# The first batch's Fourier sums in five PSUM banks, zero products in its waits, its later adds beside the first FFN

## The chip, the core and the metric

One core of a Trainium2 chip. The time is device time of one execution in microseconds (us); less is better. The engines are TensorE (PE, with its weight loads as PEld), VectorE (DVE), ScalarE (ACT), GpSimd (POOL) and SyncE (SP, which issues most DMAs). Each engine runs its own instructions strictly in order and waits on semaphores for the others.

## The reference

Three stages on B=4 sequences of S=576 tokens with 512 features, all in float32:

```
x  = softmax(mask128(q k^T / 8) + alibi) v          # 8 heads of 64, window of 128 keys
u  = x + real(fft(fft(x, over tokens), over features))
un = (u - mean(u)) / sqrt(var(u) + 1e-6)
y  = u + relu(un @ w_ch1) @ w_ch2                   # 512 -> 2048 -> 512
out[b, s] = p[e] * (relu(y[s] @ w1[e]) @ w2[e])     # e: one of 8 experts, by a gate that may keep the last e
```

The weights `w_ch1` and `w_ch2` come as 64-bit floats.

## The kernel before

Products that must be exact to float32 are made as three products of split operands: `split(hi, lo, src)` rounds `src` to `hi` on ACT and subtracts on DVE or POOL to get `lo`, and `mm3` multiplies hi by hi (L169), hi by lo (L170) and lo by hi (L171).

**The opening** (`opening()`) treats batch 0 alone, in an order written out by hand for PE, DVE, ACT and POOL. PE starts on products of a zero tile (`warm`, L306). Then comes `attention(0)`: ten units (two groups of four heads, five query tiles), each with score products on PE (L363), a masked scaling and a minimum on DVE (L367, L369, L371), four exponentials on ACT (L378), a transpose on PE (L387) copied by ACT (L391), selections on POOL (L392, L394), value products on PE (L406), a copy on DVE (`ot`, L412 and L414), and a transpose back with a scaling by the reciprocal of the sums into the rows `x` (L426 to L434). The stages of several units overlap.

Then comes `mixing(0)`. A sequence's 576 rows lie as three tile pairs `xs[kt]` (row s beside row 576-s). `fold(kt)` adds and subtracts the pair's halves and then mirrored columns on DVE (L471 to L480); `zprod` multiplies the folded tiles by the table `tab1` on PE (`zps`, L494), summed over kt; ACT copies the sums to `Z` (L498). For each of three row blocks kb, PE multiplies by `tab2` (`pz`, `pc`, L517, L518), ACT copies `pz` (L521), and DVE forms difference and sum (L522, L523) and adds them, straight and mirrored, to the rows x (L527, L528). The first halves of tile pairs 0 and 1 are normalised (`normalise`: statistics L634, a chain of small DVE operations L643 to L663, scaling on ACT L668), transposed and split (`transpose_split`) to `xT`. That is the input of the first FFN.

**The conversion** of the 64-bit weights (`load_weights64`, `values32`): ACT scales the high word (L264), DVE shifts the low word right by 29 (L265), merges the two (L266) and puts the sign in (L267), ACT and POOL split the result into `t1` and `t2` (L165, L166). Pieces go by pairs through two buffers `t64`, each free again when POOL has subtracted. Chunk 0 is converted in the opening, chunks 1 to 3 beside the first FFN.

**The first half of the FFN** (`mlp_first`) runs over nine groups of two row tiles, each with eight hidden blocks: 12 products into `hps`, relu on ACT (`h`, L580) and its rest on DVE (L583), then two `mm3` into `acc`. Beside it run attention and mixing of batches 1 to 3. What goes where is set by lanes, each with a start, a length and a count of steps; a scheduler then orders the engines. A group's successor is normalised at the steps `STEPS` of its FFN. After that come the second FFN half with routing, and the experts.

Of the kernel before, what the change touches and what calls it, by code (L numbers as in the profile page):

```python
# [23 lines left out]
DM = H * D  # L24
# [20 lines left out]
WARM = 24  # L45
FILL = 14
# [16 lines left out]
STEPS = (0, 3, 4, 9, 11)  # L63
# [94 lines left out]
def build(ctx, tc, a, out):  # L158
# [5 lines left out]
    def split(hi, lo, src, eng=None):  # L164
        nc.scalar.copy(hi, src)  # L165
        (eng or nc.vector).tensor_tensor(out=lo, in0=src, in1=hi.bitcast(F32), op=ALU.subtract)  # L166
# [69 lines left out]
    def load_weights64(chunks, i, c, wp, words):  # L236
        q = CB // 2
        ms = []
        for j in range(2):
            ms.append(values32(raws[c][j], words))  # L240
            if j == 0:
                yield
# [6 lines left out]
        for j in range(2):  # L249
            ms.append(values32(raws[c][2 + j], words))  # L250
            if j == 0:
                yield
# [6 lines left out]
    def values32(r, words):  # L259
# [31 lines left out]
    def load_part(b, g, part, pieces=1):  # L291

        t = qk.tile([P, 2, QK], F32, tag="qk", name="qkt")
        n = 2 // pieces
        for x in range(pieces):
            nc.sync.dma_start(out=t[:, x * n:(x + 1) * n], in_=a["qk"][b, g, part, :, x * n:(x + 1) * n])
        v = sm.tile([P, 3, 4 * D], F32, tag="v", name="vt", bufs=QB)
        last["load"] = nc.sync.dma_start(out=v, in_=a["v"][b, g, part].rearrange("p k h d -> p k (h d)"))
        return t, v

    raw0 = load_part(0, 0, 0, 2)
# [5 lines left out]
    ident = keep.tile([P, P], F32, name="ident")  # L307
    nc.sync.dma_start(out=ident, in_=a["ident"])
    turn = cst.tile([P, P], F32, name="turn")
    nc.vector.tensor_copy(turn, ident[:, ::-1])  # L310
    half = keep.tile([P, TM], F32, name="half")
    nc.vector.memset(half, -0.5)
    inner = keep.tile([P, 2], F32, name="inner")
    nc.sync.dma_start(out=inner, in_=a["inner"])
    first = cst.tile([P, P], BF16, name="first")
    nc.sync.dma_start(out=first, in_=a["first"])
    mask = cst.tile([P, P], I32, name="mask")
    nc.sync.dma_start(out=mask, in_=a["mask"])
    bias = cst.tile([P, 2, 4, P], BF16, name="bias")
    nc.sync.dma_start(out=bias, in_=a["bias"].rearrange("p g h x c -> p g (h x) c"))  # L320
    id16 = cst.tile([P, P], BF16, name="id16")
    nc.sync.dma_start(out=id16, in_=a["id16"])
    mixed = [-1]
    xss = {}
# [7 lines left out]
    def attention(b):  # L332
# [108 lines left out]
        for u in range(len(units) + VL + 1):  # L441
# [15 lines left out]
            yield  # L457

    def mixing(b):
        xs = xss.pop(b)  # L460
        rows = [(P, P), (P, P), (33, 32)]
        zin = []

        def fold(kt):
            n, m = rows[kt]
            xa, xb = xs[kt][:, 0], xs[kt][:, 1]
            xf = slab([P, 2, DM], F32, "xf", "m", MB)
            xe, xo = xf[:, 0], xf[:, 1]
            if kt == 0:

                nc.vector.scalar_tensor_tensor(out=xe, in0=xb, scalar=inner[:, 0:1], in1=xa, op0=ALU.mult, op1=ALU.add)  # L471
            else:
                nc.vector.tensor_tensor(out=xe[0:m], in0=xa[0:m], in1=xb[0:m], op=ALU.add)
            o = 64 if kt == 2 else 0
            nc.vector.tensor_tensor(out=xo[o:o + m], in0=xa[0:m], in1=xb[0:m], op=ALU.subtract)
            if kt == 2:
                nc.vector.tensor_copy(xe[32:33], xa[32:33])
                nc.vector.memset(xo[o + 32:o + 33], 0.0)
# [31 lines left out]
        for kb in range(3):  # L510
# [33 lines left out]
            if kb == 2:  # L544
                mixed[0] = b
# [803 lines left out]
```

## Time and profile before

| | |
|---|---|
| median of 3 runs | 980.03 us (977.93 to 981.56) |
| the profiled execution | 980.93 us, its span 978.9 us |
| PE busy | 910.6 us, 93% of the span |
| DVE, ACT, POOL busy | 53%, 38%, 24% |

The span is what the engines' records cover; the 2.0 us around it are start and end of the execution. Times of single instructions are from this one execution. An instruction that follows another of its engine without a pause starts some 0.08 to 0.1 us before the end shown for the other, so starts, not durations, give the pace.

### The profile page before, as it was taken

How to read it: one execution, taken by the hardware profiler on the slowest of the kernel's cores; microseconds unless marked ns; L12 is line 12 of the kernel's file. 1: busy time of each engine (PE TensorE's matmuls, PEld its weight loads, DVE VectorE, ACT ScalarE, POOL GpSimd, SP SyncE). 2: the span in 40 equal slices, each digit the busy share in tenths (PEclk: the TensorE clock that was granted, in tenths of full speed). 3: DMA queues.
4: the chain of work that ended last, by engine and by line, in shares of the span. 5: the costliest groups of instructions: out<-in, count | busy, mean ns of one | idle time of the engine just before them, and what ended most of it. 6: DMA issues, size and time to landing. Idle time of an engine off the chain costs nothing. (4 is left out here: it accounts for less than half of the span.)

```text
span 978.9 us, 16130 instructions
## 1 busy us (share of the span) xinstructions
PE 910.6 (93%) x5878; PEld 752.2 (77%) x5879; DVE 521.8 (53%) x1332; ACT 369.8 (38%) x974; POOL 239.7 (24%) x364
## 2 busy tenths in 40 slices
PE   8868899989999999999999999998979999999993
PEld 4535677667778797889888888887758899988782
DVE  5787866745554658521333435357546545565410
ACT  5635363543553246421111111114235445455410
POOL 2315441231221137310111313123023211222100
PEclk9989799979999999999999999999988999999997
DMA  9923071341312396253444342536167555455100
GB/s 324 378 86 108 1 238 61 121 130 52 114 66 69 120 313 194 65 151 65 108 108 108 85 110 44 120 85 194 57 188 247 186 162 164 165 189 196 64 20 20
DMA packets 109036, 129.14 MB, mean 132 GB/s; under 512 B 16222, under 2 KB 78046, under 8 KB 108884
## 3 DMA queue, kind: packets, MB, share of 16 engines
q1 hardware_dynamic: 83636, 103.95, 33.3%
q0 software_dynamic: 22720, 19.36, 9.1%
q10 hardware_dynamic: 2592, 4.72, 1.3%
q8 instruction: 48, 0.79, 0.3%
q14 instruction: 40, 0.33, 0.1%
HBM read 99.65 MB, written 30.87 MB: 133 GB/s over the span
## 5 line engine op out<-in xcount | busy, mean ns | idle before, releaser
L580 ACT ACTIVATE h<-hps 128x256 fp32r<-128x256 f32 x152 | 58.2, 383 | 262.3 <-PE hps L171 259.0
L583 DVE SCALAR_TENSOR_TENSOR h<-hps,h 128x256 fp32r<-128x256 f32 x152 | 63.8, 420 | 160.0 <-ACT h L580 160.0
L169 PE MATMUL acc<-t,h 128*128 128x512 f32 x304 | 125.8, 416 | 3.0 <-ACT h L580 3.0
L171 PE MATMUL acc<-t,h 128*128 128x512 f32 x304 | 121.7, 400 | 1.5 <-DVE h L583 1.2
L170 PE MATMUL acc<-t,h 128*128 128x512 f32 x304 | 121.9, 401 | 1.0 <-POOL t L166 0.9
L166 DVE TENSOR_TENSOR t<-we,t 128x512 fp32r<-128x512 f32 x128 | 84.5, 694 | 46.9 <-ACT t L165 46.9
L169 PE MATMUL hps<-xT,t 128*128 128x256 f32 x288 | 87.0, 302 | 4.8 <-ACT t L165 3.5
L165 ACT CAST t<-we 128x512 fp32r<-128x512 f32 x128 | 73.4, 618 | 42.4 <-DMA we<-in_w 17.9
L171 PE MATMUL hps<-xT,t 128*128 128x256 f32 x288 | 84.7, 294 | 3.5 <-POOL t L166 3.5
L169 PE MATMUL hps<-xTe,t 128*128 128x320 f32 (+7 forms) x288 | 86.4, 301 | 0.6 <-ACT xTe L165 0.6
L170 PE MATMUL hps<-xTe,t 128*128 128x320 f32 (+7 forms) x288 | 86.0, 299 | 0.0
L171 PE MATMUL hps<-xTe,t 128*128 128x320 f32 (+7 forms) x288 | 85.8, 298 | 0.0
L170 PE MATMUL hps<-xT,t 128*128 128x256 f32 x288 | 83.9, 291 | 0.0
L169 PE MATMUL hps<-xTb,t 128*128 128x256 f32 x288 | 83.6, 290 | 0.0
L170 PE MATMUL hps<-xTb,t 128*128 128x256 f32 x288 | 82.3, 286 | 0.0
L171 PE MATMUL hps<-xTb,t 128*128 128x256 f32 x288 | 82.3, 286 | 0.0
L378 ACT ACTIVATE t<-t,mx 128x128 f32<-128x128 f32 (+1 forms) x160 | 62.6, 393 | 45.7 <-DVE mx L371 41.3
L171 PEld LDWEIGHTS acc<-t,h 128*128 128x128 f32 x304 | 57.8, 190 | 17.9 <-DVE h L583 5.0
L169 PEld LDWEIGHTS acc<-t,h 128*128 128x128 f32 x304 | 58.1, 192 | 14.8 <-ACT h L580 3.2
L169 PEld LDWEIGHTS hps<-xT,t 128*128 128x128 f32 x288 | 56.8, 197 | 12.5 <-ACT t L165 4.4
L170 PEld LDWEIGHTS acc<-t,h 128*128 128x128 f32 x304 | 58.2, 191 | 9.8 <-POOL t L166 2.8
L583 DVE SCALAR_TENSOR_TENSOR hE<-hps,hE 128x256 fp32r<-128x256 f32 (+4 forms) x96 | 30.8, 349 | 62.6 <-ACT hE L580 62.1
(280 smaller groups left out, 2018.3 us busy)
## 6 DMA issues: line engine op xcount, KB each, us to landing
we<-in_w SPq DMA_DIRECT2D x64, 512.0 KB
rw<-in_w_ch SPq DMA_DIRECT2D x32, 512.0 KB
qkt<-in_qk SPq DMA_DIRECT2D x15, 642.0 KB
nd<-xT SPq DMA_DIRECT2D x18, 512.0 KB
xTb<-nd POOLq DMA_DIRECT2D x18, 512.0 KB, 6.8
vt<-in_v SPq DMA_DIRECT2D x16, 384.0 KB
pd<-y ACTq DMA_DIRECT2D x18, 256.0 KB
ub<-ud SPq DMA_DIRECT2D x18, 256.0 KB
```

The costliest lines, as they stand in the source:

```text
L165: nc.scalar.copy(hi, src)
L166: (eng or nc.vector).tensor_tensor(out=lo, in0=src, in1=hi.bitcast(F32), op=ALU.subtract)
L169: nc.tensor.matmul(o, lhsT=wh, rhs=xh, start=start, stop=False, **kw)
L170: nc.tensor.matmul(o, lhsT=wh, rhs=xl, start=False, stop=False, **kw)
L171: return nc.tensor.matmul(o, lhsT=wl, rhs=xh, start=False, stop=stop, **kw)
L378: nc.scalar.activation(t[0:m, j], t[0:m, j], AF.Exp, bias=mx[0:m, j:j + 1], scale=-1.0, accum_out=sums[0:m, j:j + 1])
L580: last["relu"] = nc.scalar.activation(h[:, 0:n], hps[:, 0:n], AF.Relu)
L583: last["rest"] = nc.vector.scalar_tensor_tensor(out=h[:, lo:lo + c1 - c0], in0=hps[:, c0:c1], scalar=0.0, in1=h[:, c0:c1].bitcast(F32), op ...
```

## The change

- The first loads stand in another order: half of the first `qkt`, `first` and `id16` come first. There are 16 warm products instead of 24, and `turn` is made on POOL.
- In attention of batch 0, from its last units on, two products of the zero tile (`spin`, 28 in all) stand behind each transpose and each value product; `FILL`, now 18 products, stands behind the `tab2` products.
- The folds of tile pairs 2 and 1 begin inside attention, pair 0 comes last; the odd half of pair 2 has 32 rows instead of 33, with the single row's copy on ACT and no memset.
- The five sums of `zprod` have five banks of their own (of the score tile, of both FFN sums and of the hidden tile) and are taken in the order 2, 1, 0, the cosine sums first.
- Only two row blocks are combined in the opening, and of each only the half that is normalised there. The other adds, row block 2 and the rows' stores are a lane of their own (`rest`, `REST`).
- `early64` scales the high words and takes the low word's top three bits (from its top byte) on ACT, for all four chunks (32 ACT instructions in the opening; before, 14 of L264 stood there and 2 behind it); DVE's shift L265 is gone.
- `normalise` makes both tiles' `u` first (in the opening one on ACT, one on DVE) and transposes afterwards; it has one step more, so `STEPS` has too.

```
-WARM = 24
-FILL = 14
+WARM = 16
+FILL = 18
+SPIN_ = 2
+REST = (25.5, 4)
-STEPS = (0, 3, 4, 9, 11)
+STEPS = (0, 3, 5, 10, 11, 13)
...
+    def early64(c):
+        for r in raws[c]:
...
+            nc.scalar.activation(w[:, :, :, 1].bitcast(F32), w[:, :, :, 1].bitcast(F32), AF.Copy, scale=BIAS)
+            yield
+            nc.scalar.activation(w[:, :, :, 0], top, AF.Copy, scale=1.0 / 32, bias=-31.0 / 64)
+            yield
...
-        nc.scalar.activation(y.bitcast(F32), y.bitcast(F32), AF.Copy, scale=BIAS)
-        nc.vector.tensor_single_scalar(t, wl, 29, op=ALU.logical_shift_right)
-        nc.vector.scalar_tensor_tensor(out=t, in0=y, scalar=3, in1=t, op0=ALU.logical_shift_left, op1=ALU.bitwise_or)
+        if not small:
+            nc.scalar.activation(y.bitcast(F32), y.bitcast(F32), AF.Copy, scale=BIAS)
+            nc.vector.tensor_single_scalar(wl, wl, 29, op=ALU.logical_shift_right)
+        nc.vector.scalar_tensor_tensor(out=t, in0=y, scalar=3, in1=wl, op0=ALU.logical_shift_left, op1=ALU.bitwise_or)
...
+    def spin(n):
...
+        for _ in range(n):
+            nc.tensor.matmul(idle[0], lhsT=id16, rhs=z16, start=True, stop=True)
...
                 flip(u - FL)
+                if b == 0 and u >= len(units) - 1:
+                    spin(SPIN_)
             if VL <= u < len(units) + VL:
                 values(u - VL)
+                if b == 0 and u >= len(units) - 1:
+                    spin(SPIN_)
...
-        for i, g in enumerate(gs):
-            with behind() if later else nullcontext():
-                un = act.tile([P, DM], F32, tag="u", name="u", bufs=UB)
-                nc.scalar.activation(un, src[i], AF.Identity, scale=v[:, 1, i:i + 1], bias=v[:, 2, i:i + 1])
-                transpose_split(xT, i * P, un)
+        us = []
+        with behind():
+            for i in range(n):
+                us.append(act.tile([P, DM], F32, tag="u", name="u", bufs=UB))
+                nc.scalar.activation(us[i], src[i], AF.Identity, scale=v[:, 1, i:i + 1], bias=v[:, 2, i:i + 1])
+        yield
+        for i, g in enumerate(gs):
+            with behind():
+                transpose_split(xT, i * P, us[i])
...
+        bank = {(0, 0): s2[:, 1], (0, 1): a2[0], (0, 2): s2[:, 0], (1, 0): a2[1], (1, 1): h1}
...
+        zprod(2)
+        words.step(2)
+        folding(1)
+        zprod(1)
+        folding(1)
+        zprod(0, (0,))
...
+        kb0 = combine(xs, Z, 0)
+        next(kb0)
+        kb1 = combine(xs, Z, 1)
+        next(kb1)
+        spin(FILL)
+        nrm = prepare(0, (xs[0][:, 0], xs[1][:, 0]))
+        words.step(8)
...
+        def rest():
+            for kb, it in ((0, kb0), (1, kb1), (2, combine(xs, Z, 2))):
+                for _ in it:
+                    yield
+                store(0, xs, kb)
+                yield
...
+    lanes.append(lane(REST[0], REST[1], 8, late_(rest)))
```

How the order moves is seen at two places. The first is ACT in the opening, from the sums' copies to the copy of the second `pz`. Before (the twelve scalings L264 stand ahead of this, two more in it):

```order
L264 ACTIVATE rw<-rw 128x512 x12
L498 COPY z_743<-zps 128x289
...
L378 ACTIVATE t,sums<-t,mx 128x128 x3
L498 COPY z_743<-zps 128x289
L498 COPY z_742<-zps 128x289
L264 ACTIVATE rw<-rw 128x512
L165 CAST t_797<-t_777 128x4x128
L165 CAST t_797<-t_792 128x4x128
L521 COPY cmb<-pz 128x258 x2
```

And of the change, from the last of the 19 instructions of `early64` (L243, L245 in turn) that stand ahead of the sums' copies, which are now L900:

```order
L243 ACTIVATE rw<-rw 128x512
L900 COPY z_749<-zps 128x289 x2
L541 CAST zn<-zps 1x289
L900 COPY z_750<-zps 128x289 x2
L245 ACTIVATE rw<-rw 128x512
L243 ACTIVATE rw<-rw 128x512
L245 ACTIVATE rw<-rw 128x512
L167 CAST t_786<-t_772 128x4x128 x2
L529 COPY cmb<-pz 128x258
```

The attention of batch 1 (L378) is gone from this stretch, and 22 instructions of `early64` stand ahead of the weights' casts where 14 of L264 stood.

The second place is DVE in the first FFN, behind the rest of its first hidden block (L583, now L634). Before:

```order
L265 TENSOR_SCALAR t_1089<-rw 128x512
L583 SCALAR_TENSOR_TENSOR h<-hps,h 128x256
L266 SCALAR_TENSOR_TENSOR t_1089<-rw,t_1089 128x512
L265 TENSOR_SCALAR t_1118<-rw 128x512
L267 SCALAR_TENSOR_TENSOR t_1089<-rw,t_1089 128x512
L266 SCALAR_TENSOR_TENSOR t_1118<-rw,t_1118 128x512
L267 SCALAR_TENSOR_TENSOR t_1118<-rw,t_1118 128x512
L367 COPY_PREDICATED s<-mask,s 128x4x128
```

And of the change (the conversion is L281 and L282, the moved adds are L535 and L536, the scores' scaling and minimum L397 and L399):

```order
L634 SCALAR_TENSOR_TENSOR h<-hps,h 128x256
L535 TENSOR_TENSOR x<-x,cmb 128x257
L536 TENSOR_TENSOR x<-x,cmb 128x255
L397 SCALAR_TENSOR_TENSOR t<-s,bias 128x512
L281 SCALAR_TENSOR_TENSOR t_960<-rw 128x512
L399 TENSOR_REDUCE mx<-t 128x4
L634 SCALAR_TENSOR_TENSOR h<-hps,h 128x256
L282 SCALAR_TENSOR_TENSOR t_960<-rw,t_960 128x512
L535 TENSOR_TENSOR x<-x,cmb 128x257
L536 TENSOR_TENSOR x<-x,cmb 128x255
L530 TENSOR_TENSOR cmb<-pc,cmb 33x258
```

The conversion of a piece has two rows instead of three, and the adds and more of batch 1's attention stand between them. Between the first and the eighth row of the hidden rest, DVE had 12 of L265, 26 of L266 and L267 and 4 score groups (L369 with L371, most with L367); it now has 22 of L281 and L282, 8 score groups and 10 adds (eight into x, two that form difference and sum).

## Rows read from the trace of the kernel before

**Rows 1.** The page: busy time of the engines.
```profile
PE 910.6 (93%) x5878; PEld 752.2 (77%) x5879; DVE 521.8 (53%) x1332; ACT 369.8 (38%) x974; POOL 239.7 (24%) x364
```
**Rows 2.** Stretches: length; busy PE, PEld, DVE, ACT, POOL (instructions); clock, DMA.
```profile
8.46:45.60 37.14, 30.39 (x312) 21.58 (x311) 28.46 (x71) 24.84 (x97) 13.32 (x29) 1.00 1.03 374
45.60:80.20 34.60, 26.22 (x117) 14.30 (x116) 28.40 (x73) 15.74 (x45) 3.74 (x4) 0.85 0.37 130
80.20:139.50 59.30, 49.82 (x311) 37.72 (x310) 45.61 (x80) 27.89 (x83) 31.29 (x42) 0.88 0.33 106
139.50:200.00 60.50, 58.56 (x461) 42.81 (x460) 41.97 (x95) 29.77 (x115) 15.69 (x36) 1.00 0.33 108
```
**Rows 3.** Timeline of PE to the first FFN (start, duration, idle before).
```profile
1.26 7.37 PE L306 MATMUL warm<-z 128*128 128x512 bf16 x24 [1.26 <-DVE carry L877]
...
45.59 3.18 PE L788 MATMUL fill<-bias,id 128*128 128x512 bf16 x13
...
69.90 1.55 PE L363 MATMUL s<-qkt 64*65 64x193 f32 x8 [5.88 <-DVE v L643]
73.61 1.11 PE L552 MATMUL tps<-ident,u 128*128 128x128 f32 x4 [2.16 <-ACT u L668]
...
80.21 0.39 PE L169 MATMUL hps<-xT,t 128*128 128x256 f32 x1
```
**Rows 4.** Timeline of DVE, from the folds to the normalising.
```profile
46.44 0.75 DVE L471 SCALAR_TENSOR_TENSOR xf<-x,inner 128x512 f32<-128x512 f32 x1
...
53.18 0.42 DVE L480 TENSOR_TENSOR xf<-xf 33x255 f32<-33x255 f32 x1
...
62.11 0.43 DVE L522 TENSOR_TENSOR cmb<-pc,cmb 128x258 f32<-128x258 f32 x1 [1.53 <-ACT cmb L521]
...
62.78 1.36 DVE L527 TENSOR_TENSOR x<-x,cmb 128x257 f32<-128x257 f32 x1
...
67.08 1.27 DVE L634 BATCH_NORM_STATS2 st<-x 128x6 f32<-128x512 f32 x2
...
72.55 0.16 DVE L663 SCALAR_TENSOR_TENSOR v<-mv,v 128x2 f32<-128x2 f32 x1
```
**Rows 5.** Timeline of ACT in the Fourier stage.
```profile
42.08 6.87 ACT L264 ACTIVATE rw<-rw 128x512 f32<-128x512 f32 x12
...
57.85 0.70 ACT L498 COPY z<-zps 128x289 f32<-128x289 f32 x2 [0.21 <-PE zps L494]
...
60.66 1.14 ACT L165 CAST t<-t 128x512 fp32r<-128x512 f32 x2 [1.54 <-DVE t L267]
61.71 0.64 ACT L521 COPY cmb<-pz 128x258 f32<-128x258 f32 x2
...
72.74 0.81 ACT L668 ACTIVATE u<-x,v 128x512 f32<-128x512 f32 x1 [0.59 <-DVE v L663]
```
**Rows 6.** Waits from 80.2 to 139.5 us: in total, times, longest.
```profile
DVE t L265 <- POOL t L166: 9.2, 7, 2.5
PE hps L171 <- POOL t L166: 3.5, 3, 2.3
PE hps L169 <- ACT t L165: 3.5, 3, 1.3
```
**Rows 7.** DVE's conversions from 80.2 to 139.5 us, and a pair of POOL's subtractions.
```profile
L265 DVE TENSOR_SCALAR t<-rw 128x512 uint32<-128x512 uint32 x14 | 11.1, 801 | 9.2 <-POOL t L166 9.2
L266 DVE SCALAR_TENSOR_TENSOR t<-rw,t 128x512 uint32<-128x512 uint32 x14 | 9.5, 698 | 0.0
...
104.03 1.50 DVE L265 TENSOR_SCALAR t<-rw 128x512 uint32<-128x512 uint32 x1 [0.73 <-POOL t L166]
...
61.36 2.50 POOL L166 TENSOR_TENSOR t<-t,t 128x512 fp32r<-128x512 f32 x2 [2.61 <-ACT t L165]
102.72 2.53 POOL L166 TENSOR_TENSOR t<-t,t 128x512 fp32r<-128x512 f32 x2 [1.59 <-ACT t L165]
```
**Rows 8.** Timeline of PE: the transposes of a later group's rows.
```profile
201.85 0.65 PE L552 MATMUL tps<-ident,u 128*128 128x128 f32 x4 [2.45 <-ACT u L668]
```

More of the change, by code (lines that the diff above doesn't have):

```diff
@@ L499, in zprod @@
                 else:
-                    nc.scalar.copy(zn[0:1, 0:K1], ps[0:1, 0:K1])
-                    nc.vector.tensor_tensor(out=zn[32:33, 0:K1], in0=ps[0:1, 0:K1], in1=zn[0:1, 0:K1].bitcast(F32), op=ALU.subtract)
+                    low_row(ps[0:1, 0:K1], slice(0, K1))
         for kt in range(3):
-            fold(kt)
+            for xf in fold(xs, kt):
+                pass
+            zin.append(xf)
             zprod(parts[0], kt)
@@ L732, in conversions @@
     def conversions():
-        for c in range(FA // CB):
-            yield from load_weights64(chunksA, c, c, wpA, lambda: sm.tile([P, 2 * CB], U32, tag="t64", name="t64", bufs=2))
+        for c in range(1, FA // CB):
+            yield from load_weights64(chunksA, c, c, wpA, lambda: sm.tile([P, 2 * CB], U32, tag="t64", name="t64", bufs=2), soon64[c])
     END = object()
@@ L768, in mix, with folding @@
         yield from mixing(b)
+    soon64 = [None] * nA
     conv = conversions()
     def opening():
+        xs = None
+        folds, got = [], {}
+        def folding(n):
+            for _ in range(n):
+                for kt, it in folds:
+                    r = next(it, False)
+                    if r is not False:
+                        if r is not None:
+                            got[kt] = r
+                        break
+        words = Beside()
         for n, _ in enumerate(attention(0)):
@@ L778, in opening @@
                 load_raw(0, wpA)
+                soon64[0] = early64(0)
+                words.add(soon64[0])
             if n == 14:
@@ L781, in opening @@
                     load_raw(c, wpA)
-        attended.add(0)
-        ends = [last[x].ins for x in ("x", "w", "pool")]
-        xs = xss[0]
-        fill = ps_h1.tile([P, DM], F32, tag="h", name="fill")
-        for _ in range(FILL):
-            nc.tensor.matmul(fill, lhsT=id16, rhs=bias[:, 0].rearrange("p h c -> p (h c)"), start=True, stop=True)
-        m = mixing(0)
-        for _ in range(3):
-            next(m)
-        next(conv)
-        next(m)
-        next(conv)
-        next(m)
+                    soon64[c] = early64(c)
@@ new lines, in opening @@
+                    words.add(soon64[c])
+            xs = xss[0]
+            if n == 23:
+                folds.append((2, fold(xs, 2)))
+                folding(1)
+            if n >= 24:
+                words.step(2)
+            if n == 25:
+                folding(1)
+                folds.append((1, fold(xs, 1)))
+            if n == 26:
+                folding(1)
+        attended.add(0)
+        folds.append((0, fold(xs, 0)))
+        folding(1)
+        idle[0] = None
+        h1 = ps_h1.tile([P, DM], F32, tag="h", name="zps")
@@ new lines, in copies @@
+        def copies(cs):
+            for db in range(2):
+                nc.scalar.copy(Z[cs][:, db], bank[cs, db][:, 0:K1])
+        zprod(2)
+        words.step(2)
+        folding(1)
+        zprod(1)
+        folding(1)
+        zprod(0, (0,))
+        words.step(1)
+        folding(1)
+        q = CB // 2
+        room0 = [wraw.tile([P, 4 * CB], U32, tag="r64", name="t64", bufs=RB) for _ in range(2)]
+        place = iter([t[:, x * 2 * CB:(x + 1) * 2 * CB] for t in room0 for x in range(2)])
@@ new lines, in opening, with value @@
+        ms = []
+        def value():
+            ms.append(values32(raws[0][len(ms)], lambda: next(place), True))
+        copies(0)
+        value()
+        low_row(bank[0, 2][0:1, 0:K1], slice(0, K1))
+        zprod(0, (1,))
+        copies(1)
+        value()
+        t1 = wpA.tile([P, 2, 4, CB], F32R, tag="w1", name="t1")
+        for j in range(2):
+            split(t1[:, 0, :, j * q:(j + 1) * q], t1[:, 1, :, j * q:(j + 1) * q], ms[j], nc.gpsimd)
+        kb0 = combine(xs, Z, 0)
+        next(kb0)
```

225 lines of the change are left out of this document (136 added, 89 removed).

## The prediction

> **What bounds the kernel now.** I read the page first: PE is busy for 910.6 us of 978.9 [rows 1], so what can be won lies in the 68.3 us of its idle time and in products that run at a low clock. A table of busy time by stretch says where these are. From 45.6 to 80.2 us PE is busy for 26.22 of 34.6 us, at a granted clock of 0.85 of full speed on average (the levels are 1.2 and 2.4 GHz); from 80.2 to 139.5 for 49.82 of 59.3, at 0.88; from there to 200 for 58.56 of 60.5, at 1.00 [rows 2]. So the Fourier stage of batch 0 and the first FFN lose 8.4 and 9.5 us in idle time and some more in slow products, and behind them PE itself is the bound. What is saved before 139.5 us is kept to the end, if the order behind it stays, and the orders of the two kernels say that it does, but for the steps of the normalising.
>
> Next the timelines of that stage. In the Fourier stage a serial chain sets the end. The folds run on DVE from 46.44 to 53.6 us [rows 4]; the last copies of the sums end on ACT at 58.55; ACT copies the first `pz` only at 61.71, behind two casts for which it had waited 1.54 us (DVE's conversion) [rows 5]. DVE combines from 62.11 to 67.1, normalises until 72.7 [rows 4], ACT scales the first tile from 72.74 [rows 5], and the first FFN product comes at 80.21. In this time PE stands still for 5.88 us before 69.90 and 2.16 before 73.61, and a transposition of four blocks then takes 1.11 us, against 0.65 later [rows 3, 8].
>
> In the first FFN the waits say that PE waits for POOL's and ACT's halves of the converted weights, 3.5 us for POOL alone, and DVE for POOL to free a buffer, 9.2 us in 7 times [rows 6]. The chain there is: POOL subtracts, DVE converts the next pair, ACT rounds it, POOL subtracts.
>
> **The change part by part.** I follow the chain, with the times of before.
>
> *Start.* Eight of 24 warm products go, which take 7.37 us together [rows 3]. The last ones are the fast ones; 13 products of the same width later take 3.18 us, 0.23 each [rows 3], so the eight are worth 1.9 us. The first scores need `first` and `id16`, whose loads move from the fifth and the eighth place to the second and the third, so they need not hold the scores. I take -1.7; bounds 0 (a load is late) and -1.9.
>
> *Zero products in attention.* 28 products of 0.23 us are 6.4 us. PE is idle for 6.7 us of the 37.1 of attention [rows 2], so most of them fill time in which it waits. Where one stands directly ahead of value products whose copy DVE is waiting for, it delays; in the last two units that is two pairs of 0.46. I take +0.9; bounds 0 and +6.4. The clock is 1.00 in all of attention already [rows 2], so there they win nothing.
>
> *Folds.* From the first fold to the last DVE spends 7.2 us behind the last row of attention [rows 4]. Now six of its instructions are left there (two of pair 1, four of pair 0): at the mean of the 14 that stood there, 0.51, they take 3.1 us. Four others, 2.0 us, stand just ahead of the last row; part of that fills idle time of DVE (8.7 us of attention's 37.1 [rows 2]), and I let them push the row by 1.3. The folds end 2.8 us earlier than they did, and 13 of their 15 products need not wait for the last one.
>
> *Copies of the sums.* What is late next is ACT. Ahead of these copies stand 19 instructions of `early64`. No row shows the one with the bytes; its bounds are the 0.35 us of a copy of 289 columns (two in 0.70) and double the 0.57 that the scaling L264 takes (12 in 6.87) [rows 5]. I take 0.57, since it writes as many elements in the same stride. 19 of them are 10.9 us. They start where L264 started at 42.08, some 0.4 us later for the copied row, and so end at 53.4, less 1.7, plus 0.9: 52.6. Four copies and the small one (0.35 each at the pace of the row) end at 54.4 where they ended at 58.55: -4.1 so far. Were the byte form to take double, the nine of them here would add 5.1 us.
>
> *To the first combined block.* Three more of `early64` (1.7 us), two casts (1.05) and the copy of `pz`: it starts at 57.2, against 61.71: -4.5.
>
> *Combining and normalising.* DVE did twelve adds from 62.11 to 67.08 [rows 4]; eight stand there now. One of the twelve took 1.36, the others share 3.6, 0.33 each; with that one kept, the eight take 3.7 us, so the statistics begin at 61.2 (-5.9). From there the chain took 5.6 us to 72.7, with three wide instructions of batch 1's attention within (2.1 us by L266's 0.70 [rows 7], less what overlaps, some 1.8); these are gone: 65.0 (-7.7).
>
> *Scaling, transposing.* Before, the second tile came behind the first, and between them stood a row block's products and adds: 72.74 to 80.21, 7.5 us [rows 3, 5]. Now ACT and DVE scale one tile each (0.81), PE transposes eight blocks, at the slow clock of before 2.2 us [rows 3], and ACT rounds the second (0.6): 3.6 us. The first FFN product comes at 69.0 us, 11.2 earlier. I take the slow transposes because PE still stands idle ahead of them: the 18 zero products (4.1 us) end some 3 us before the scaled tiles do.
>
> *The first FFN.* Gone from DVE between the first and the eighth hidden block are 12 instructions of L265, 0.80 us each on average [rows 7], and four merges of 0.70: 12.4 us. In their place come 10 adds at 0.33 (3.3 us) and the attention of batch 1 that used to stand in the opening, four score groups of three wide instructions at 0.70 (8.4): 11.7. DVE's work is nearly the same; PE's grows by the scores and by row block 2, some 6 us, in a stretch in which it has 9.5 us idle. I take its 59.3 us as unchanged. Bounds: -9.2 (DVE's waits for POOL all go, since other work lies between) and +9.5 (each of the ten adds waits for POOL, below).
>
> *Later groups.* Both scaled tiles now exist before either transposition. One wait of this kind is 2.45 us [rows 8]; but the second transposition now stands nearer to the group's end. I take -0.4; bounds -2.45 and +1.2 (a rounding and a subtraction that come too late once).
>
> Sum: -11.2 + 0 - 0.4 = -11.6 on the profiled execution's 980.93 (2.0 more than its span): 969.3. The execution lies 0.9 above the median of the runs, so in medians 968.4; I say 968.5. A measurement can tell about 0.5%, 4.9 us, from no change.
>
> **The rivals.**
>
> *The port (the first FFN gives half back).* While POOL subtracted from 61.36 to 63.86, an add of x and cmb, both in SBUF, took 1.36 us on DVE where the others go on after 0.33 [rows 4, 7]; L265 took 1.50 beside the pair from 102.72, against a mean of 0.80 [rows 7]. So such an add can be held up by about 0.95, taking a free one at 0.4 with its end. The Trainium skill's page "SBUF — State Buffer" ("Who interferes with whom") has this as a rule: a DVE instruction with two inputs in SBUF, or in its two-port mode, and a POOL instruction that reads SBUF exclude each other for their whole length. By that rule, L281, with both inputs in SBUF, waits behind the second subtraction of a pair just as L265 did. As a mechanism of this kernel: the ten adds move from a stretch with 3.74 us of POOL's work into one with 31.29 [rows 2], and each pair's first L281 stays held up by about 1. If half of the adds are hit, +4.8, and the first FFN takes 64: 973.3. All ten hit, +9.5: 978.0. For it: the 9.2 us of waits show that DVE and POOL take turns. Against it: a pair has one held-up instruction as before and two fewer instructions.
>
> *ACT is the chain.* If the byte form costs double, the nine put the copies off by 5.1 us; the other seven stand ahead of the scaling, where ACT is done at 63.7 in the sum above and is waited for at 65.0. Then all sixteen cost 9.1, less that slack: +7.8, 976.3. For it: 32 instructions on ACT where 14 were; against it: no row says that such a read is slower.
>
> *Nothing comes of it.* The first FFN is fed by the conversion alone; if its chain is not shorter and starts no earlier than POOL's and ACT's other work lets it, the 11 us turn into waits for weights: 978 to 982. Against it: the chain's first pairs follow the same start, as chunk 0's do.
>
> *The other side: slower.* Every two-input DVE instruction of the first FFN pays for POOL: the 24 of L281 and L282 for chunks 1 to 3, and the 10 adds. Held up by 0.95 each beyond what is paid today, the 34 are +32: 1000. It decides from 18 of the 34 on: 17 us is what was won and 4.9 more, 985.6. For it: POOL is busy for half of the stretch; against it: L266, with both inputs in SBUF, has a mean of 0.70 in it [rows 7], so it is hardly ever held up.
>
> *More than forecast.* DVE's waits are filled by the adds and the scores: 9.2 us less, 959.
>
> **How the numbers follow.** Forecast 0.60, with its own range from 964 to 973 (the Fourier chain uncertain by 3 us to either side, the first FFN by 2); the port 0.15; ACT 0.08; nothing 0.07; slower 0.05; more 0.05. Faster by over 0.5% means below 975.1: the forecast, more, and two thirds of the port: 0.75, and a little of ACT, 0.76. Slower means above 985: 0.05, and 0.01 of "nothing". The rest, 0.18, is the same. The range from 962 to 977 takes in the forecast, most of the port and ACT, and leaves out "nothing", "slower" and the best cases, some 0.18.
>
> **What would show it.** The first FFN product near 69 us; ACT's sums' copies at 52 to 53, directly behind `early64` with no idle time ahead of them; the first combine near 57.5; no DVE instruction on conversions but two for a piece; the first FFN 57 to 62 us long with a first L281 of 1.1 us or more over its usual time in each pair; from its end on the same intervals as before. I am wrong if the first FFN takes over 66 us, if the copies of the sums come after 56, or if the stretches behind 200 us differ by more than 2 us.

## The result: 969.03 us, 1.2% faster

The changed kernel takes 969.03 us (median of 4 runs, 967.68 to 969.35), the kernel before 980.79 beside it (4 runs, 977.93 to 982.75): a ratio of 0.988 [0.984, 0.992]. Run once more with the last experiments it took 969.67 (6 runs). The profiled execution took 969.35, with a span of 967.6. The forecast of 968.5 and the sign were right; several of its terms were not, and they made up for one another, so that it came this close is partly luck.

The page, against [rows 1], shows PE with the same work in a span that is 11.3 us shorter:

```profile
PE 909.6 (94%) x5889; PEld 751.8 (78%) x5889; DVE 513.5 (53%) x1308; ACT 379.7 (39%) x993; POOL 241.1 (25%) x365
```

The table of stretches, with the columns of [rows 2]: from the last row of attention to the first product of the first FFN, that FFN, and the stretch behind it.

```profile
46.20:71.30 25.10, 22.42 (x95) 12.61 (x93) 19.11 (x49) 20.15 (x39) 2.52 (x2) 0.91 0.25 97
71.30:131.30 60.00, 51.02 (x334) 37.17 (x334) 47.81 (x85) 31.07 (x103) 31.94 (x44) 0.92 0.44 134
131.30:192.00 60.70, 59.94 (x465) 43.81 (x463) 40.17 (x92) 31.32 (x119) 14.87 (x33) 1.00 0.34 110
```

In the first stretch PE stands still for 2.7 us; in the corresponding one of before it was 8.4 [rows 2]. The first FFN still loses 9 us of idle time and some at a slow clock, and behind it PE is again the bound.

The trace has fourteen `spin` products, not the 28 named above: of their line (L350) there are 32, and 18 of these are `FILL`.

The timeline of PE to the first FFN, as in [rows 3]:

```profile
6.70 0.28 PE L387 MATMUL s<-first,id 128*128 128x128 bf16 x2
...
15.58 1.12 PE L434 MATMUL o<-w,vt 128*64 128x128 f32 x8 [1.72 <-POOL w L420]
16.64 2.08 PE L391 MATMUL s<-qkt 64*128 64x256 f32 x8
...
46.21 0.28 PE L459 MATMUL xps<-sums,turn 128*128 128x4 f32 x2
46.43 10.22 PE L896 MATMUL zps<-tab,xf 33*128 33x289 f32 x30
...
68.73 1.09 PE L603 MATMUL tps<-ident,u 128*128 128x128 f32 x8 [2.68 <-ACT u L723]
69.75 1.59 PE L525 MATMUL pc<-tab,z 128*33 128x258 f32 x4
71.27 0.58 PE L171 MATMUL hps<-xT,t 128*128 128x256 f32 x1
71.78 1.92 PE L525 MATMUL pz<-tab,z 128*33 128x258 f32 x4
73.63 0.39 PE L172 MATMUL hps<-xT,t 128*128 128x256 f32 x1
```

The first FFN product comes 8.9 us earlier (80.21 before [rows 3]). Of the lead of 1.76 us at the first scores, 1.1 is left at the first value products, for which PE waits 1.72 us, and nothing behind the eight slow scores that follow them (2.08 us). Two lots of `tab2` products stand around the first hidden product, slow, so the second comes 2.4 us behind it. The thirty products of the sums now run without a pause, in 10.2 us, at a clock of 0.84 (46.2 to 56.6 us). Before, they stood behind the `fill` products [rows 3] and took 7.7 us in three lots, at a clock of 1.00 (45.6 to 57.8 us):

```profile
48.60 1.75 PE L494 MATMUL zps<-tab,xf 128*128 128x289 f32 x6
...
50.70 1.82 PE L494 MATMUL zps<-tab,xf 128*128 128x289 f32 x6
...
53.66 4.16 PE L494 MATMUL zps<-tab,xf 33*128 33x289 f32 x18
```

The chain beside it, on ACT and on DVE, as in [rows 4, 5]; two fences, one for each engine.

```profile
49.36 0.66 ACT L245 ACTIVATE rw<-rw 128x512 uint32<-128x512 uint8 x1
49.92 0.66 ACT L243 ACTIVATE rw<-rw 128x512 f32<-128x512 f32 x1
50.49 0.67 ACT L245 ACTIVATE rw<-rw 128x512 uint32<-128x512 uint8 x1
...
55.51 0.70 ACT L900 COPY z<-zps 128x289 f32<-128x289 f32 x2 [1.59 <-PE zps L896]
...
59.71 0.36 ACT L529 COPY cmb<-pz 128x258 f32<-128x258 f32 x1
...
67.86 0.81 ACT L723 ACTIVATE u<-x,v 128x512 f32<-128x512 f32 x1 [1.38 <-DVE v L714]
```
```profile
51.59 0.42 DVE L509 TENSOR_TENSOR xf<-xf 128x255 f32<-128x255 f32 x1
...
60.11 0.43 DVE L530 TENSOR_TENSOR cmb<-pc,cmb 128x258 f32<-128x258 f32 x1 [1.70 <-ACT cmb L529]
...
60.79 1.39 DVE L535 TENSOR_TENSOR x<-x,cmb 128x257 f32<-128x257 f32 x1
...
63.77 1.27 DVE L685 BATCH_NORM_STATS2 st<-x 128x6 f32<-128x512 f32 x2
...
67.67 0.16 DVE L714 SCALAR_TENSOR_TENSOR v<-mv,v 128x2 f32<-128x2 f32 x1
```

ACT stands idle for 1.59 us ahead of the copies of the sums, and the releaser is PE. The instruction on bytes (L245) goes at the pace of the one beside it, 0.56 from start to start.

In the first FFN, POOL, DVE and PE around 100 us, and DVE's conversions of the whole stretch, as in [rows 6, 7]; a fence for each:

```profile
97.61 0.23 POOL L694 TENSOR_SCALAR v<-mv 128x2 f32<-128x2 f32 x1
...
101.22 0.24 POOL L703 TENSOR_SCALAR v<-v 128x2 f32<-128x2 f32 x1
...
102.33 2.50 POOL L168 TENSOR_TENSOR t<-t,t 128x512 fp32r<-128x512 f32 x2
```
```profile
76.33 1.52 DVE L536 TENSOR_TENSOR x<-x,cmb 128x255 f32<-128x255 f32 x1
...
103.63 2.36 DVE L281 SCALAR_TENSOR_TENSOR t<-rw 128x512 uint32<-128x512 uint32 x2 [3.60 <-POOL t L168]
```
```profile
103.65 0.38 PE L173 MATMUL hps<-xT,t 128*128 128x256 f32 x1 [3.15 <-POOL t L168]
```
```profile
L281 DVE SCALAR_TENSOR_TENSOR t<-rw 128x512 uint32<-128x512 uint32 x13 | 14.5, 1127 | 6.4 <-POOL t L168 6.4
```

POOL's twelve small operations for the second group's reciprocal root stand ahead of a subtraction; DVE waits 3.60 us and PE 3.15 for it. An add at 76.33, 0.41 when free, is held up, and L281 has a mean of 1.13 us.

### The profile page after: what moved, and what is told of

The parts are those of the page before. It is cut to its first block, busy times and chain, and to the rows that moved or that the text cites. A ratio compares the mean times of both kernels' runs of the same rounds, so it can differ in the third digit from the quotient of the medians.

```text
span 967.6 us, 16131 instructions
## 1 busy us (share of the span) xinstructions
PE 909.6 (94%) x5889; PEld 751.8 (78%) x5889; DVE 513.5 (53%) x1308; ACT 379.7 (39%) x993; POOL 241.1 (25%) x365
## 5 line engine op out<-in xcount | busy, mean ns | idle before, releaser
L634 DVE SCALAR_TENSOR_TENSOR h<-hps,h 128x256 fp32r<-128x256 f32 x152 | 63.7, 419 | 170.0 <-ACT h L631 169.9
L171 PE MATMUL hps<-xT,t 128*128 128x256 f32 x288 | 85.5, 297 | 2.5 <-ACT t L167 2.2
L173 PE MATMUL hps<-xT,t 128*128 128x256 f32 x288 | 83.1, 289 | 4.2 <-POOL t L168 4.2
L172 PE MATMUL hps<-xT,t 128*128 128x256 f32 x288 | 83.1, 289 | 0.0
L171 PEld LDWEIGHTS acc<-t,h 128*128 128x128 f32 x304 | 57.7, 190 | 15.5 <-issue 4.4
L634 DVE SCALAR_TENSOR_TENSOR hE<-hps,hE 128x256 fp32r<-128x256 f32 (+4 forms) x96 | 30.8, 349 | 61.4 <-ACT hE L631 60.4
```

The lines of the kernel that those rows point to most:

```text
L171: nc.tensor.matmul(o, lhsT=wh, rhs=xh, start=start, stop=False, **kw)
L172: nc.tensor.matmul(o, lhsT=wh, rhs=xl, start=False, stop=False, **kw)
L173: return nc.tensor.matmul(o, lhsT=wl, rhs=xh, start=False, stop=stop, **kw)
L634: last["rest"] = nc.vector.scalar_tensor_tensor(out=h[:, lo:lo + c1 - c0], in0=hps[:, c0:c1], scalar=0.0, in1=h[:, c0:c1].bitcast(F32), op ...
```

## The experiments

One table gives the readings of the profiled executions on which the verdicts rest, in us: the start of the last row's sums on PE (end of attention), the first hidden product, the time between, the time from the second hidden product to the first copy of `y` (the first FFN), the start of the last copy of `y` in the first half, how long the thirty products of the sums took, and the median of the runs with its ratio to the kernel before. The experiments ran on three chips, so the ratio, taken with the kernel before on the same chip, compares better than the median.

| kernel | last row | hidden | between | first FFN | last y | sums | median | ratio [95%] |
|---|---|---|---|---|---|---|---|---|
| before | 45.44 | 80.21 | 34.8 | 57.2 | 453.6 | 7.7 | 980.79 | |
| after | 46.21 | 71.27 | 25.1 | 57.7 | 444.9 | 10.2 | 969.03 | 0.988 [0.984, 0.992] |
| after, again (e12) | 46.92 | 72.15 | 25.2 | 57.7 | 445.2 | 10.2 | 969.67 | 0.990 [0.986, 0.994] |
| e1 old normalise | 46.69 | 71.17 | 24.5 | 61.5 | 449.3 | 8.6 | 973.40 | 0.993 [0.990, 0.996] |
| e2 no zero products | 48.70 | 73.83 | 25.1 | 57.8 | 448.6 | 10.2 | 974.15 | 0.998 [0.995, 1.001] |
| e3 FILL 30 | 47.01 | 71.95 | 24.9 | 60.8 | 447.1 | 10.2 | 970.09 | 0.990 [0.983, 0.997] |
| e4 `alt` late | 44.52 | 70.08 | 25.6 | 57.7 | 443.0 | 10.2 | 967.83 | 0.987 [0.980, 0.994] |
| e5 shifts on DVE | 47.80 | 71.86 | 24.1 | 63.1 | 448.8 | 8.6 | 976.94 | 0.997 [0.993, 1.001] |
| e6 root on DVE | 46.33 | 70.71 | 24.4 | 56.8 | 442.8 | 8.6 | 967.25 | 0.987 [0.981, 0.993] |
| e7 adds early | 47.91 | 73.81 | 25.9 | 57.4 | 445.9 | 8.6 | 970.33 | 0.991 [0.988, 0.993] |
| e8 = e4 and e6 | 43.77 | 66.71 | 22.9 | 56.9 | 438.5 | 8.6 | 966.69 | 0.988 [0.982, 0.995] |
| e9 folds late | 46.49 | 74.29 | 27.8 | 60.0 | 448.9 | 11.8 | 974.22 | 0.994 [0.991, 0.997] |
| e10 block 2 between | 46.81 | 73.97 | 27.2 | 59.4 | 447.4 | 8.6 | 972.52 | 0.992 [0.989, 0.996] |
| e11 = e8, more runs | 44.65 | 70.05 | 25.4 | 55.8 | 439.5 | 10.2 | 966.00 | 0.987 [0.982, 0.992] |

Where an experiment leaves attention alone, its last row still lies anywhere from 46.3 to 47.9, so smaller differences there mean nothing. The interval behind it depends on the clock: the thirty products of the sums take 8.6 us at full clock or 10.2 where it falls among them, though the order up to there is the same (after and e6, for example). Why it falls in one execution and not in the other was not found. So intervals compare only at the same time for the sums: with 10.2 they lie from 24.9 to 25.6; with 8.6 from 24.1 to 24.5 (e1, e5, e6), 22.9 in e8, 25.9 in e7 and 27.2 in e10, and these last two are discussed below. By the ratios only e2 and e5 lie outside the interval of after; for the others the times of whole runs decide nothing, and the readings at the place of the edit do. The order of the first loads, the five banks and the move of batch 1's attention were not undone apart.

**The zero products in attention** (e2):
```
-SPIN_ = 2
+SPIN_ = 0
```


> The changed kernel without the 28 zero products in the tail of attention (SPIN_ 0; the 18 ahead of the normalising stay). Theory (the clock is at its upper level there anyway, and the products delay the last value products): attention's last row comes 0.5 to 1 us earlier and the first FFN product with it; the time is 968 to 969 us. Rival (they hold the clock up): the granted clock falls below 0.95 between 34 and 50 us, the sums' products are slower, and the first FFN product comes 1 us or more later, 970 us.

The rows of stretches of this run:
```profile
18.70:34.00 15.30, 14.34 (x146) 10.85 (x145) 12.86 (x32) 9.11 (x37) 5.00 (x11) 0.91 0.94 330
34.00:46.00 12.00, 9.38 (x82) 6.97 (x78) 6.63 (x21) 6.18 (x22) 4.90 (x10) 0.72 1.05 384
```
The mean clock is 0.72 from 34 to 46 us; in the changed kernel it is 1.00 there, and so it is in every other profiled execution with these products. The last row is the latest of all, 2.5 us behind that of after and 0.8 behind the latest of the others, and the median is 5 us more (ratio to before 0.998 [0.995, 1.001]). The rival is right: in this kernel these products (fourteen, not 28) hold the clock. It is no rule for every kernel: before had 1.00 without them (its clock in [rows 2]), with a pause of 1.64 us ahead of 38.35 where e2 has one of 1.65 ahead of 38.98, and why was not tested.

**The start** (e4): POOL converts `alt` at unit 14 instead of at unit 4.
```
-        nc.gpsimd.tensor_copy(alt, alt32)
+        return alt32
...
             if n == 14:
+                nc.gpsimd.tensor_copy(alt, alt32)
```


> The changed kernel with POOL's cast of the table alt ten half steps of attention later, so that POOL does not wait for its load (0.74 us at 13.8 us) ahead of the first selection. Theory (the 1.76 us by which the first scores come earlier are lost there: the first value products wait 1.72 us for POOL, and the clock falls to 0.67 in the stretch behind): the first value products come at about 14.8 instead of 15.6 us, the clock stays up, and the fourth unit's scores end 1 to 2 us earlier; attention ends 1 us or more earlier and the time is 967.5 to 968.5 us. Rival (the lead is lost to DVE or to loads later in attention): the first value products are earlier, but attention ends where it did, 969 us.

The cast on POOL in the changed kernel:
```profile
14.53 0.40 POOL L788 CAST alt<-alt 128x258 fp32r<-128x258 f32 x1 [0.74 <-DMA alt<-in_alt]
```
Without it there, the first value products wait half as long and run fast:
```profile
15.29 0.66 PE L434 MATMUL o<-w,vt 128*64 128x128 f32 x8 [0.86 <-POOL w L420]
15.87 1.13 PE L391 MATMUL s<-qkt 64*128 64x256 f32 x8
```
Eight scores take 1.13 us where the changed kernel took 2.08. The three kernels with this edit (e4, e8, e11) have their last row at 43.8 to 44.7, the others with zero products at 46.2 to 47.9. In the changed kernel, then, a cast that waited 0.74 us for its DMA ahead of POOL's first selection, with the slow products that followed, cost the whole lead of the start. The time of whole runs does not show it (0.987 against 0.988).

**The folds** (e9): all of them behind the last row.
```
             if n == 23:
                 folds.append((2, fold(xs, 2)))
-                folding(1)
...
-        folding(1)
+        folding(4)
```


> The changed kernel with the folds of tile pairs 2 and 1 taken out of attention again: all fold work stands behind the last row, still in the order 2, 1, 0. Theory (the early folds are worth about 2, four fold halves of 0.5 each): the last row of attention comes 0 to 1.3 us earlier, and from it to the first hidden product it takes 26.5 to 28 us instead of 25.1; the whole is 0.5 to 2 us more, 969.5 to 971. Rival (the sums' thirty products on PE, at the slow clock, are what the copies wait for, and the folds have slack): the interval stays 25.1 within 0.5, and the whole is 967.5 to 969.

```profile
46.49 0.28 PE L459 MATMUL xps<-sums,turn 128*128 128x4 f32 x2
48.61 11.82 PE L892 MATMUL zps<-tab,xf 33*128 33x289 f32 x30 [1.84 <-DVE xf L506]
```
PE waits 1.84 us for the first fold, and the products behind the pause take 11.8 us instead of 10.2. DVE is done with the folds 2.1 us later (its next instruction starts at 54.06, after: 51.93). The interval is 27.8: the early folds are worth 2.7. The last row, at 46.49, lies between those of the two executions of the changed kernel (46.21 and 46.92), so no push is seen. The first FFN is 2.3 longer too, at a clock of 0.89 (after: 0.94), and the median is 5 more than after, more than the theory said; the intervals of the two ratios just meet.

**Two tiles together** (e10): the opening scales the second tile on ACT behind the first, and row block 2 is back between their transpositions.
```
             for i, g in enumerate(gs):
+                nc.scalar.activation(un, src[i], AF.Identity, ...)
                 transpose_split(xT, i * P, un)
...
+        for _ in kb2:
+            pass
```


> The changed kernel with the normalising of the opening as it was: both tiles scaled on ACT one after the other, and row block 2's products and adds back between the transpositions of the first tile and of the second. Theory (the largest single piece, 4.1 of the 9.7 us by which the first hidden product came nearer to the last row, is that nothing stands between the two tiles): the interval from the last row to the first hidden product is 28.5 to 30 us instead of 25.1, the first FFN from its second product 1 to 2 us shorter, the whole 970 to 973. Rival (the clock or PE's earlier products gave that piece, not the order): the interval is under 27 us and the whole 968 to 970.

```profile
66.86 0.81 ACT L719 ACTIVATE u<-x,v 128x512 f32<-128x512 f32 x1 [1.39 <-DVE v L714]
...
71.77 0.81 ACT L719 ACTIVATE u<-x,v 128x512 f32<-128x512 f32 x1
```
From the first scaling to the first hidden product it takes 7.1 us, 3.4 after and 7.5 before [rows 3, 5]: the piece is where the theory put it. The interval is only 27.2 because the sums ran at full clock in this execution (8.62 us for the thirty, 10.22 after). So the price is 3.7 at its place. The first FFN did not get shorter; it has a wait of 3.2 us for a selection of POOL that after does not have, and a clock of 0.86. The profiled execution, at 979.56 us, is the longest of the nine, so that stretch says little.

**The adds** (e7): the remaining adds of row blocks 0 and 1 ahead of the normalising. They are four, not six as the expectation says: from the first difference to the statistics stand twelve instructions instead of eight.
```
+        for it in (kb0, kb1):
+            for _ in it:
+                pass
         spin(FILL)
```


> The changed kernel with the six adds of row blocks 0 and 1 that it had put beside the first FFN done ahead of the normalising again. Theory (such adds cost 0.41 each when free, and beside POOL only few of them are held up by about 1): the statistics begin 2 to 2.5 us later, the first hidden product comes near 73.5 instead of 71.3, and the first FFN is shorter by no more than 1.5; the whole is 969 to 972. Rival (the port: adds beside POOL's subtractions cost about 1 us more each): the first FFN shortens by 3 us or more from its second product, and the whole is 968 or less.

```profile
60.21 0.43 DVE L530 TENSOR_TENSOR cmb<-pc,cmb 128x258 f32<-128x258 f32 x1 [1.70 <-ACT cmb L529]
...
65.21 1.27 DVE L685 BATCH_NORM_STATS2 st<-x 128x6 f32<-128x512 f32 x2
```
The first FFN is 57.4 long, 0.3 less: four adds beside it cost next to nothing. In the opening they cost 1.3: from the first difference to the statistics it takes 5.00 us, after 3.66. The interval, 0.8 longer than after, hides part of this, since the sums ran at full clock here; against e1, e5 and e6 it is 1.4 to 1.8 longer. The rival, the port, is not borne out as a cost of the moved adds, though of the six adds that stayed beside the first FFN two were held up (1.41 and 1.51 us).

**The shifts** (e5): DVE shifts again, ACT only scales.
```
-            nc.scalar.activation(w[:, :, :, 0], top, AF.Copy, ...)
...
+        nc.vector.tensor_single_scalar(wl, wl, 29, op=ALU.logical_shift_right)
```


> The changed kernel with one part undone: DVE shifts the low words right by 29 in place again, and ACT only scales (16 instructions fewer on ACT, 16 more on DVE, four of them in the opening and twelve beside the first FFN). Theory (the shifts are worth little by themselves, since DVE has idle time beside the first FFN and POOL's subtraction is what is waited for): in the opening ACT is earlier by up to 5 us but PE, not ACT, was late at the copies, so these stay where they are within 0.5 us; DVE has 1.5 to 3 us more ahead of the first hidden product, and the first FFN, counted from its second product to its first y copy, takes 57 to 62 us; the whole 966 to 974. Rival (the chain of the conversion sets the first FFN's pace and the shifts were part of it): twelve shifts of 0.8 lengthen it by about 9 us, to 67, and the whole is 977 or more.

The stretch from the second hidden product to the first y, here, in the changed kernel and before:
```profile
74.00:137.10 63.10, 49.15 (x328) 36.60 (x328) 51.99 (x93) 31.16 (x104) 34.12 (x44) 0.95 0.40 122
```
```profile
73.60:131.30 57.70, 48.72 (x329) 36.37 (x329) 45.51 (x81) 31.07 (x103) 31.94 (x44) 0.94 0.43 132
```
```profile
81.34:138.60 57.26, 47.78 (x300) 36.28 (x300) 43.75 (x77) 26.19 (x81) 31.29 (x42) 0.88 0.34 107
```
Against the changed kernel, DVE has twelve instructions and 6.5 us more, PE the same work at the same clock, and the stretch is 5.4 longer. My theory fell: the conversion's chain through DVE does set this stretch, at more than half of the rival's 9 us.

In the opening ACT now has time to spare, and the copies of the sums still wait for PE. The same copies and their thirty products in e1, which has all of `early64`, stand below:
```profile
55.50 0.70 ACT L899 COPY z<-zps 128x289 f32<-128x289 f32 x2 [4.46 <-PE zps L895]
```
```profile
54.38 0.70 ACT L896 COPY z<-zps 128x289 f32<-128x289 f32 x2
```
```profile
46.90 8.62 PE L892 MATMUL zps<-tab,xf 33*128 33x289 f32 x30
```
Both ran their sums at full clock, and in both the copies start 7.7 us behind the last row's sums (47.80 and 46.69); in e1 ACT comes to them directly from `early64`. After, with the clock down, it was 9.3. So at full clock ACT and PE are ready at the same time, and what PE is late in the changed kernel's profile is the price of the clock.

**The normalising of later groups** (e1) as before, each tile scaled and transposed in one step:
```
-STEPS = (0, 3, 5, 10, 11, 13)
+STEPS = (0, 3, 4, 9, 11)
```


> The changed kernel with the later groups' normalising as before: each tile is scaled and transposed in turn, and STEPS is the old list. Theory (the opening gives 7.2 us by the end of the first FFN, the split normalising gives the 2.5 to 2.7 us that come in the second group): the first FFN's end stays at 131.3 us, PE waits again some 2.5 us for a scaled tile in the second group, the lead over the kernel before falls from 9.9 back to about 7.3 us behind that group, and the time is about 971.6 us. Rival (the second group's wait went because its work stands elsewhere in time): the wait stays away and the time is 969 us, within 1.

The waits of PE from 139 us to the end of the first half, here and in the changed kernel:
```profile
PE tps L603 <- ACT u L734: 5.4, 4, 2.5
```
```profile
PE o L434 <- POOL v L700: 2.5, 1, 2.5
PE tps L603 <- ACT u L735: 2.2, 1, 2.2
```
The four waits come back, 5.4 us against 4.7 in two. From the first y to the last of the first half it takes 315.3 us, after 313.6: 1.7 of the 4.4 by which the medians differ (the intervals of the ratios overlap). The larger part lies in the first FFN, 3.8 us longer (its second product came 1.1 earlier), and is the clock:
```profile
72.50:134.00 61.50, 53.28 (x329) 39.40 (x329) 45.68 (x82) 31.07 (x104) 30.88 (x44) 0.89 0.41 128
```
As many products (329) keep PE busy for 53.28 us instead of 48.72. Whether the steps' order brought this about or only this execution had it is open.

**More filling** (e3):
```
-FILL = 18
+FILL = 30
```


> The changed kernel with 30 zero products instead of 18 ahead of the normalising; 12 more are 2.6 us, about as long as PE stands still before the transposes (2.68 us). Theory (the clock falls because of that pause, 0.75 and 0.58 from 69 to 74 us): the clock stays at 1.00 through the transposes, the third row block's products take half as long, and the second FFN product comes at about 72 instead of 73.6 us; 967 to 968 us, if the first FFN keeps its length. Rival (the fall comes from elsewhere, or the products push the transposes back): the second FFN product at 73.6 us or later, 969 us or more.

```profile
69.52 1.09 PE L603 MATMUL tps<-ident,u 128*128 128x128 f32 x8 [0.50 <-ACT u L723]
...
71.95 0.38 PE L171 MATMUL hps<-xT,t 128*128 128x256 f32 x1
...
72.82 0.39 PE L172 MATMUL hps<-xT,t 128*128 128x256 f32 x1
```
Of the pause 0.50 is left, and the second hidden product is 0.9 behind the first, not 2.4. But the first FFN took 60.8, at a clock of 0.89, and nothing is left in the time.

**The wait at 103 us** (e6): the second group's reciprocal root on DVE.
```
+        pool = later and j != 1
-        eng = nc.gpsimd if later else nc.vector
+        eng = nc.gpsimd if pool else nc.vector
```


> The changed kernel with the second group's chain for the reciprocal root on DVE instead of POOL, so that POOL's subtraction for the next weights does not stand behind it (it ran 97.6 to 102.3 us there, and DVE waited 3.60 and PE 3.15 behind the subtraction). Theory (POOL's queue makes that pause, and the slow clock behind it costs more): the wait of PE near 103 us goes, the first FFN from its second product takes 54 to 56 us instead of 57.7, the whole is 2 to 4 us less, 965 to 967. Rival (the pause is that of the weights' chain as such and only moves): another wait of 2 to 3 us appears within the same stretch, and the time is 968 to 970; if the chain on DVE puts DVE late instead, up to 972.

```profile
100.58 0.39 PE L173 MATMUL hps<-xT,t 128*128 128x256 f32 x1 [0.52 <-POOL t L168]
```
The wait of 3.15 is 0.52, and the clock from 100 to 130 us is 1.00 (0.94 after). The first FFN takes 56.8, 0.9 less, where 54 to 56 was expected: waits of 0.67 (for DVE's `h`) and 0.52 (POOL) follow within 7 us. The median, 967.25, alone shows no gain over after (0.987 against 0.988).

**Both edits** (e8, and e11 with more runs beside the changed kernel, e12):

> Two edits on the changed kernel together: POOL's conversion of the alternating table is moved from ahead of the first selections to behind the fourteenth unit, as in the run before, and the second group's chain for the reciprocal root stands on DVE. Theory: both gains add, 1.7 for the first and 2 to 4 for the second: 962 to 966. Rival: the second wins nothing or only where the clock falls changes: 967 to 969.

> The two edits together once more (the alternating table converted behind the fourteenth unit, the second group's chain for the reciprocal root on DVE), in more runs, beside the changed kernel itself on the same chip. If both gains are real: 964 to 967, the interval of the ratio below that of the changed kernel. If the earlier difference was chance: 968 to 969, as the changed kernel.

> The changed kernel itself, beside the run with both edits: 968 to 970 if its first result stands.

e11: 966.00 us (963.39 to 970.92), ratio to before 0.987 [0.982, 0.992]; e12: 969.67 (967.08 to 970.96), 0.990 [0.986, 0.994]. e8: 966.69. The version with both edits is faster than the kernel before. Against the changed kernel on the same chip it is 3.7 us less in the median, but the intervals overlap, and e8's ratio, 0.988, is that of after, so a gain over the changed kernel is not shown. Its first half ends 5.7 us earlier in the profile (439.5 against 445.2).

## Why the prediction was right

By its own steps, on the profiled executions:

- *Start* (-1.7): measured -1.76 at the first scores. At the first value products 1.1 was left, and at the last row of attention the kernel was 0.8 late. The step that failed is that the lead would carry through: POOL's cast of `alt` and the slow products behind it took it (e4).
- *Zero products* (+0.9, "there they win nothing"): wrong in sign. Without them the clock falls and the last row is 0.8 to 2.5 later than with them (e2). I read the clock of 1.00 before as something that the new order would keep. There are fourteen and not 28, so the upper bound is 3.2 and not 6.4.
- *Folds* (-2.8, and 1.3 for the push on the row): the gain is real, 2.1 on DVE and 2.7 in the interval (e9); no push is seen. These three misses cancel by luck: the sum put the last row 0.5 late, it was 0.8 late.
- *Copies of the sums*: this step failed. I named ACT as late next, with its copies from 52.6 behind `early64` and no idle time. They started at 55.51 after 1.59 idle, on PE, whose thirty products ran from 46.43 at a clock of 0.84 (a stretch from 46.2 to 56.6). ACT's price was right (0.56 apiece for the byte form, taken as 0.57); it was done at 53.9, 1.3 later than forecast, chiefly because the start's lead had not lasted. The other 1.6 is PE: I reckoned when folds and ACT were done, and gave the products of the sums (thirty; I wrote of 15) no time and no clock. At full clock that would have cost nothing (e1, e5); at the clock of this execution it made PE the late one. The copies end at 57.1 instead of 54.4, and 2.3 of the 2.7 are left at the first hidden product, 71.27 instead of 69.0.
- *Combining, normalising, scaling*: 3.66 us from the first difference to the statistics (3.7 forecast, with the one add held up to 1.39 as in [rows 4]), 4.1 from there to the end of the chain (3.8), 3.4 to the first hidden product (4.0, though the terms given make 3.6). In the last, two misses offset each other: the eight transposes took 1.09 us where 2.2 was forecast, and four `tab2` products (1.59), which had no term, stood between them and the first hidden product. e10 shows this last piece apart.
- *First FFN, unchanged*: from its second product 57.7, before 57.2; from its first, 1.7 longer, since slow `tab2` products part the two. DVE is busy in it for 45.51 us, before for 43.75 (the rows stand in e5): 1.8 more, where 0.7 less was forecast. The clock was 0.88 and is 0.94, so it is partly luck that the length stayed the same. The removal of the shifts mattered: without it the stretch would have been 5.4 longer (e5).
- *The port*: half there. L281, 0.67 when free, took 1.75 in five cases beside POOL's second subtraction; the 13 take 14.5 us, 5.8 more than free, and so replace L265's hold-up [rows 7]. The rule of the Trainium skill's page "SBUF — State Buffer" ("Who interferes with whom"), that such an instruction and POOL's reads exclude each other, agrees with these rows. Each of the six pairs of subtractions in this stretch held up one L281, the first pair an add as well. Of the ten adds that was the only one, at 1.52, and e7 shows that four of them cost 0.3.
- *Later groups* (-0.4): measured -1.4. The wait at 201.85 [rows 8] did not vanish; a wait of 2.50 for POOL's root stands at 202.43. The last stretch ahead of the second group's `y` had a clock of 0.78 before (200.0 to 223.6) and of 0.92 after (192.0 to 213.7).
- *Not forecast*: the second half of the kernel, whose code is the same, took 525.3 us before and 522.7 after. Over the profiled executions of all experiments it took 520.1 to 530.3, so these 2.6 can't be put down to the change. They exceed the 2 us that the prediction gave as a sign of being wrong for the stretches behind 200 us.

The sum: -8.9 to the first hidden product, +1.7, -1.4 and -2.6 make the 11.3 of the span. So -11.6 was met by luck in its parts: 2.3 and 1.7 us of gain were missing in the opening and the first FFN, and 1.0 and 2.6 came unforecast behind them. The mechanism holds for the opening: the interval from the last row to the first hidden product fell by 9.7, and of this e9 puts 2.7 to the folds, e10 3.7 to the two tiles together and e7 1.3 to the adds, while batch 1's attention, gone from the chain behind the statistics, shortened that from 5.6 to 4.1 (read, not undone). The rivals: the port has its mechanism and not its price, the double cost of bytes is refuted, and the slower case does not arise.

## What to carry to other kernels

When an edit shortens one engine's part of a chain, work out every engine's time to the same point, and TensorE's at either clock; the one that was late next here was the one that the sum left out, and only where its clock had fallen. Before comparing two profiles, compare a stretch that neither edit touches: here the thirty products differed by 1.6 us. A small operation that waits for a DMA, put ahead of the first item of an in-order queue, can cost a whole start. To move work to an idle engine pays where its old engine stood in a chain, whatever that engine's share of busy time is (5.4 us for twelve shifts on a DVE that is busy for four fifths of the stretch).

## What the runs showed of the hardware

- From 34 to 46 us the granted clock was 1.00 in every profiled execution of the changed order that had zero products in its waits, and 0.72 in the one without (e2). The kernel before had 1.00 there without them.
- The same order of instructions had its clock fall in one execution and not in another: the thirty products of the sums took 10.22 us after and 8.62 in e6.
- The clock can fall behind a pause rather than in it: after 2.68 us of idle time eight transpositions ran at full pace (1.09 us), and the products that followed took 1.59 and 1.92 for four where 1.03 is usual. With the pause cut to 0.50 us (e3) four took 1.06.
- The same 329 products of the first FFN kept PE busy for 48.72 us at a mean clock of 0.94 and for 53.28 at 0.89 (e1), with less idle time in the second case (8.2 us against 9.0).
- An ACT instruction that reads every eighth byte goes at the pace of one that reads words, 0.56 us for 128x512.
